# The first two matmuls of layer one on token halves, with two transposes meant to go between them

## The chip, the core and the metric

The kernel runs on one core of a Trainium2 chip. The metric is the device time of one execution in microseconds (us). The profile records one execution. It times from the first instruction of the program (the span, about 1.3 us shorter than the metric). TensorE has two rows in it: PE for matmuls and PEld for the weight loads that run under them (208.5 and 121.1 us busy in a span of 212.0 us, so they overlap). DVE is VectorE, ACT is ScalarE, SP is the engine that issues most loads (SPq in the lists).

## The reference, cut to what matters

For 2048 tokens of width 640 the program computes a gate, a state-space branch and a dense branch, and mixes them:

```python
x = A_x                                            # 1 x 2048 x 640
g = _sigmoid((x * gate_w).sum(-1, keepdims=True))
a = _A_ref(x, ...)        # x -> 640 complex states, scan over tokens, projection back
b = _B_ref(x, w1, b1, w2, b2)                      # gelu(x @ w1 + b1) @ w2 + b2, 640 -> 1728 -> 640
return g * a + (1 - g) * b
```

Only the first matrix product of `_B_ref`, "layer one", for the first 512 tokens is touched. It contracts over 640 input features, which are five slabs of 128. Each slab needs the matching rows of `w1` and the matching 128 rows of x transposed (features on partitions, tokens along the row).

## The kernel before

Every operation is declared with its inputs, its outputs, an assumed duration and a priority. A small list scheduler then decides each engine's order once, when the kernel is built. It does so from the *assumed* durations: at every step it takes, among the operations whose inputs are ready in its own clock, the one with the lowest priority number.

```python
def order(self):
    ...
        avail = [(it.prio, it.idx, it) for it, r in released[e] if r <= now + 1e-9]
        avail.sort(key=lambda x: (x[0], x[1]))
        it = avail[0][2]
```

The loads of the start are issued in this order. Slabs 0 and 1 of x are loaded plainly and transposed on TensorE. Slabs 2 to 4 come through a transposing load (`xtrans`).

```python
KN = 2
load("xna", "sp", "l_xna", xn[0][:, :, 0:KN * 128], ...)      # x, slabs 0 and 1
w1load(0, "sp", 1)
w1load(1, "sp", 1.3)
w1load(2, "sp", 2)
xtrans(0, range(KN, KD), 3, 1.8)                              # xT, slabs 2, 3, 4
w1load(3, "sp", 4)
w1load(4, "sp", 5)
```

A warm-up of six and a half empty matmuls keeps TensorE busy almost until x is there (in the profile of this kernel it starts at 0.78 us, its last matmul at 3.29, and the first transpose at 3.68). Then come eight 128x128 transposes into PSUM (where TensorE's results go, here eight banks `PS[0]` to `PS[7]`), three copies from PSUM to `xT`, and the forty matmuls of the first eight output tiles, slab by slab (`k`), eight tiles each (`jf`):

```python
for i, (k, c0, c1) in enumerate(((0, 0, 2), (0, 2, 4), (1, 0, 4))):   # slab, token blocks
    bank = 7 - i
    ...                                     # f_xt: TensorE transposes of these blocks into PSUM
    op(f"xt{i}", "pe", 0.11 * (c1 - c0), ["xna", "ident"], [("bank", bank)], f_xt, prio=-990 + i)
    ...                                     # f_xc: VectorE copies them to xT[0]
    op(f"xc{i}", "dve", 0.42, [("bank", bank)], [("xT", 0, k, c0)], f_xc, prio=-2000 + i)

def m1_first():
    seq = [(k, jf) for k in range(KD) for jf in range(NW)]
    seq.remove((0, NW - 1))
    seq.insert(seq.index((1, NW - 1)), (0, NW - 1))
    for k, jf in seq:

        def f_mm(jf=jf, k=k):
            return inc("pe", nc.tensor.matmul(PS[jf][:, :], W1sb[:, k, jf * 128:(jf + 1) * 128], xT[0][:, k, :],
                                              start=(k == 0), stop=(k == KD - 1)))

        op(f"m1_0_{jf}_{k}", "pe", d_mm(512), XK0[k] + [("w1", k)], [("bank", jf)], f_mm, prio=pe_prio())
```

The tile `jf = 7` of slab 0 is pushed behind the seven others of slab 1, because its PSUM bank 7 is first used for transposes.

Of the kernel before, what the change touches and what calls it, by code (L numbers as in the profile page):

```python
# [147 lines left out]
class Prog:  # L148
# [8 lines left out]
    def op(self, name, eng, dur, reads, writes, fn, prio=None, lat=0.0, after=()):  # L157
        deps = {}
        for k in reads:
            for w in self.last_w.get(k, ()):  # L160
                deps[w.idx] = w
        for k in writes:
            for w in self.last_w.get(k, ()):
                deps[w.idx] = w
            for r in self.last_r.get(k, ()):
                deps[r.idx] = r
        for a in after:
            deps[a.idx] = a
        deps = list(deps.values())
        E = self.E  # L170

        def run(eg, deps=deps, eng=eng, fn=fn):
            E.wait(eng, *[d.done for d in deps if not (eng == "pe" and d.eng == "pe")])
            return fn()

        it = self.sch.add(name, eng, dur, deps, run, prio=prio, lat=lat)
        for k in writes:
            self.last_w[k] = [it]
            self.last_r[k] = []
        for k in reads:  # L180
            self.last_r.setdefault(k, []).append(it)
        return it


def bass_gated_mix__ssm_conv_s5__dense_activation_gelu__prompt_kernel(
# [18 lines left out]
    _, S, D = A_x.shape  # L204
# [3 lines left out]
    KD = D // 128  # L208
# [17 lines left out]
    with ExitStack() as es:  # L226

        def SB(name, shape, dt):
            return es.enter_context(nc.sbuf_tensor(name, list(shape), dt))

        xT = [SB(f"xT_{i}", [128, KD, 512], BF16) for i in range(NQ)]
        xn = [SB(f"xn_{i}", [128, 4, D], BF16) for i in range(2)]
        W1sb = SB("W1sb", [128, KD, F], BF16)
# [9 lines left out]
        cols = SB("cols", [128, 3 * KP + NF], FP32)  # L243
# [10 lines left out]
        ident = SB("ident", [128, 128], BF16)  # L254
# [33 lines left out]
        PS = [es.enter_context(nc.psum_tensor(f"ps{i}", [128, 512], FP32)) for i in range(8)]  # L288
# [13 lines left out]
        op = pr.op  # L302

        def inc(eng, ins):
            return E.inc(eng, ins, eng + "_s")
# [8 lines left out]
        def d_act(n):  # L314
            return 0.26 + n * 0.00084
# [4 lines left out]
        def d_mm(n):  # L320
            return n / 2400.0 + 0.004
# [44 lines left out]
        ROWS = {"lre": (0, A_Lambda_re), "lim": (KP, A_Lambda_im), "ldt": (2 * KP, A_log_dt), "b1a": (3 * KP, B_b1[0:nmain])}  # L366
# [34 lines left out]

        op("warm", "pe", 2.7, (), [("bank", 4)], f_warm, prio=-1000)

        for i, (k, c0, c1) in enumerate(((0, 0, 2), (0, 2, 4), (1, 0, 4))):
            bank = 7 - i
            pt = PS[bank][:, :].bitcast(BF16)[:, 0:(c1 - c0) * 128]

            def f_xt(k=k, pt=pt, c0=c0, c1=c1):
                t = None
                for c in range(c0, c1):  # L410
                    t = nc.tensor.transpose(pt[:, (c - c0) * 128:(c - c0 + 1) * 128], xn[0][:, c, k * 128:(k + 1) * 128], ident[:, :])
                return inc("pe", t)

            op(f"xt{i}", "pe", 0.11 * (c1 - c0), ["xna", "ident"], [("bank", bank)], f_xt, prio=-990 + i)

            def f_xc(k=k, pt=pt, c0=c0, c1=c1):
                return inc("dve", nc.vector.tensor_copy(out=xT[0][:, k, c0 * 128:c1 * 128], in_=pt))

            op(f"xc{i}", "dve", 0.42, [("bank", bank)], [("xT", 0, k, c0)], f_xc, prio=-2000 + i)

        XK0 = [[("xT", 0, k)] for k in range(KD)]
        XK0[0] = [("xT", 0, 0, 0), ("xT", 0, 0, 2)]
        XK0[1] = [("xT", 0, 1, 0)]
        XT = {q: [("xT", q, k) for k in range(KD)] for q in range(1, NQ)}
        XT[0] = [t for x in XK0 for t in x]

# [2 lines left out]
        def f_cols():  # L429
            return inc("pe", nc.tensor.transpose(psC, rows[:, :], ident[:, :]))  # L430

        op("cols", "pe", 0.3, list(ROWS) + ["b1b", "ident"], [("bank", 7)], f_cols, prio=11.5)

        def f_cols1():
            return inc("dve", nc.vector.tensor_copy(out=cols[:, :], in_=psC[:, 0:RT + 1]))
# [147 lines left out]
        def pe_prio():  # L583
            ctr["pe"] += 1
            return ctr["pe"]
# [26 lines left out]
        def m1_first():  # L612
            seq = [(k, jf) for k in range(KD) for jf in range(NW)]
            seq.remove((0, NW - 1))
            seq.insert(seq.index((1, NW - 1)), (0, NW - 1))
            for k, jf in seq:

                def f_mm(jf=jf, k=k):
                    return inc("pe", nc.tensor.matmul(PS[jf][:, :], W1sb[:, k, jf * 128:(jf + 1) * 128], xT[0][:, k, :],  # L619
                                                      start=(k == 0), stop=(k == KD - 1)))  # L620

                op(f"m1_0_{jf}_{k}", "pe", d_mm(512), XK0[k] + [("w1", k)], [("bank", jf)] ,
                   f_mm, prio=pe_prio())
            for jf in range(NW):
                ctr["bank"] += 1

                def f_ge(jf=jf):
                    return inc("act", nc.scalar.activation(Gl[0][:, jf, :], PS[jf][:, :], ACT.Gelu_apprx_tanh, bias=b1col[:, jf:jf + 1]))

                op(f"ge_0_{jf}", "act", d_act(512), [("bank", jf), "b1col"], [("gl", 0, jf)], f_ge, prio=10)  # L630
# [248 lines left out]
        def outs(q, mid=None):  # L879
# [14 lines left out]
            comb(cs[-1])  # L894

        m1_first()
        m1(0, NW)
        bproj(0)
# [81 lines left out]
```

## Time and profile before

The time was 213.26 us (median of 3 runs).

The page of the profile, its first table and its summary of the chain that ended last (followed back from the last instruction, at each step to what released it):

```profile
span 212.0 us, 3133 instructions
PE 208.5 (98%) x1264; PEld 121.1 (57%) x1274; DVE 189.3 (89%) x263; ACT 111.3 (53%) x201; POOL 3.0 (1%) x11
...
PE 96%; DMA 2%; SPq 0%; issue 0%; DVE 0%
PE ps L769 27%; PE ps L639 22%; PE ps L818 21%; PE ps L682 20%; PE ps L619 3%; DMA W1sb<-in_B_w_dram 2%; PE ps L783 1%; PE ps L660 1%; SPq L326 0%; DVE osb L852 0%; PE ps L430 0%
```

The kernel is a row of matmuls. The only other thing on its chain of any size is a load of W1sb, 2% of the span. Line L619 is the matmul of the code above, the part that is changed, and it holds 3%.

The same chain in order of time for the start (start in us, length in us, what it was):

```profile
1.80 4.59 DMA W1sb<-in_B_w_dram
6.39 0.05 issue
6.44 1.04 PE ps L619 x4
...
8.61 0.04 issue
8.65 3.84 PE ps L619 x17
...
14.00 5.40 PE ps L639 x25
```

What lies before 6.39 us on TensorE is not on the chain at all: the chain goes through the load of W1sb slab 1. Twenty-five 512-column matmuls take 5.40 us, so one takes 0.216 us in this unbroken stretch.

The waits of the weight-load row (who waited for what, total us, times, longest), from 3 to 9 us:

```profile
PEld ps L411 <- DMA xn<-in_A_x_dram: 0.7, 1, 0.7
PEld ps L619 <- DMA W1sb<-in_B_w_dram: 0.6, 1, 0.6
PEld ps L619 <- DMA xT<-in_A_x_dram: 0.5, 1, 0.5
...
PEld ps L619 <- DVE xT L417: 0.2, 1, 0.2
```

So TensorE waits for x (until 3.68), for the second copy (until 4.68), for W1sb slab 1 (until 6.44), and for xT slab 2 (until 8.65). A weight load can be done before its matmul (the last one of slab 1 runs from 8.02 to 8.12 us, its matmul starts at 8.23), so these lengths on the weight-load row overstate the lost time. The matmul starts tell it better. The timeline in windows of a few hundredths of a microsecond shows the last matmul before each of the two later waits:

```profile
5.99 0.38 PE L619 MATMUL ps<-xT,W1sb 128*128 128x512 bf16 x1
8.23 0.38 PE L619 MATMUL ps<-xT,W1sb 128*128 128x512 bf16 x1
```

The first wait costs 6.44 - (5.99 + 0.216) = 0.23 us and the second 8.65 - (8.23 + 0.216) = 0.20 us. Whatever is delayed ahead of both waits has 0.43 us of slack in this run.

### The profile page before, as it was taken

The numbers are of one execution on the slowest core, as the hardware profiler recorded it, in microseconds if no ns is written. First come the engines' busy times: TensorE is split into PE (matmuls) and PEld (weight loads), VectorE is DVE, ScalarE is ACT, GpSimd is POOL, SyncE is SP. The second block draws the span as 40 slices with busy tenths as digits, with TensorE's granted clock in tenths as the row PEclk, the third lists the DMA queues.
The fourth block names the chain that finished last, engine by engine and source line by source line (L and its number), as shares of the span: only waits on it lengthen the run. The fifth ranks groups of instructions, "written<-read, shape, count | busy, mean of one in ns | idle before, by whom it ended". The sixth has DMA issues, their size and how long they took to land.

```text
span 212.0 us, 3133 instructions
## 1 busy us (share of the span) xinstructions
PE 208.5 (98%) x1264; PEld 121.1 (57%) x1274; DVE 189.3 (89%) x263; ACT 111.3 (53%) x201; POOL 3.0 (1%) x11
## 2 busy tenths in 40 slices
PE   8999999999999999999999999999999999999996
PEld 3344444444467776444466777544446777767775
DVE  2499999999999999999999959899999999899544
ACT  2489556678915234556953233556793444723331
POOL 2000000000000010000000001000000000000000
PEclk9999999999999999999999999999999999999999
DMA  5999799999100004100000014000000000010011
GB/s 151 310 276 206 157 231 317 261 203 180 21 0 3 31 31 127 62 0 0 0 3 0 0 34 156 31 31 3 0 0 2 3 31 31 31 34 0 31 34 62
DMA packets 31318, 16.35 MB, mean 77 GB/s; under 512 B 23112, under 2 KB 30408, under 8 KB 31304
## 3 DMA queue, kind: packets, MB, share of 16 engines
q1 hardware_dynamic: 30928, 14.83, 28.4%
q0 software_dynamic: 320, 1.31, 1.9%
q8 instruction: 10, 0.16, 0.3%
q14 instruction: 4, 0.03, 0.1%
q10 hardware_dynamic: 56, 0.01, 0.0%
HBM read 7.63 MB, written 2.62 MB: 48 GB/s over the span
## 4 chain that ended last, share of the span: by engine, by line
PE 96%; DMA 2%; SPq 0%; issue 0%; DVE 0%
PE ps L769 27%; PE ps L639 22%; PE ps L818 21%; PE ps L682 20%; PE ps L619 3%; DMA W1sb<-in_B_w_dram 2%; PE ps L783 1%; PE ps L660 1%; SPq L326 0%; DVE osb L852 0%; PE ps L430 0%
## 5 line engine op out<-in xcount | busy, mean ns | idle before, releaser
L769 PE MATMUL ps<-W2sb,Gl 128*128 128x320 bf16 x416 | 59.2, 299 | 0.0
L769 PEld LDWEIGHTS ps<-W2sb,Gl 128*128 128x128 bf16 x416 | 40.4, 98 | 17.0 <-issue 1.1
L639 PE MATMUL ps<-xT,W1sb 128*128 128x512 bf16 x215 | 47.5, 379 | 0.3
L818 PE MATMUL ps<-CT,H 128*128 128x320 bf16 (+2 forms) x330 | 45.4, 295 | 0.0
L722 DVE TENSOR_TENSOR_SCAN W<-atab,V 128x1280 bf16<-128x1280 f32 x16 | 44.3, 2811 | 0.3
L682 PE MATMUL ps<-xT,BT 128*128 128x512 bf16 x196 | 43.1, 379 | 0.3 <-issue 0.2
L818 PEld LDWEIGHTS ps<-CT,H 128*128 128x128 bf16 x330 | 32.0, 98 | 11.7
L797 ACT ACTIVATE E<-ps,g1col 128x320 bf16<-128x320 f32 x32 | 16.3, 526 | 39.7 <-PE ps L769 25.8
L639 PEld LDWEIGHTS ps<-xT,W1sb 128*128 128x128 bf16 x220 | 21.6, 98 | 25.9
L646 ACT ACTIVATE Gl<-ps,cols 128x512 bf16<-128x512 f32 x44 | 29.6, 689 | 10.0 <-PE ps L639 10.0
L682 PEld LDWEIGHTS ps<-xT,BT 128*128 128x128 bf16 x200 | 19.5, 98 | 23.4 <-ACT Gt L668 0.4
L691 ACT ACTIVATE U<-ps 128x512 bf16<-128x512 f32 x40 | 23.8, 597 | 14.9 <-PE ps L682 14.9
L829 ACT ACTIVATE E<-ps,gcol 128x320 bf16<-128x320 f32 x30 | 15.8, 528 | 22.6 <-PE ps L818 22.6
L756 ACT ACTIVATE ps<-b2b 128x320 f32<-128x320 bf16 x32 | 14.1, 442 | 1.1
L480 DVE TENSOR_TENSOR osb<-xg,E 128x640 bf16<-128x640 bf16 x15 | 7.3, 487 | 8.1 <-ACT E L829 7.8
L839 DVE SCALAR_TENSOR_TENSOR xg<-xn,gcol,dsk 128x640 bf16<-128x640 bf16 x16 | 13.9, 883 | 0.4
L596 DVE SCALAR_TENSOR_TENSOR scr<-xn,gwb 128x640 bf16<-128x640 bf16 x16 | 13.2, 823 | 0.4
L480 DVE TENSOR_TENSOR H<-H,V 128x1280 bf16<-128x1280 bf16 x16 | 12.5, 821 | 0.3
L480 DVE TENSOR_TENSOR V<-V,W 128x1280 bf16<-128x1280 bf16 x16 | 12.5, 821 | 0.3
L480 DVE TENSOR_TENSOR V<-mr,U 128x2560 bf16<-128x2560 bf16 x8 | 11.9, 1489 | 0.2
L480 DVE TENSOR_TENSOR H<-c,W 128x2560 bf16<-128x2560 bf16 x8 | 11.9, 1489 | 0.2
L480 DVE TENSOR_TENSOR V<-s,W 128x2560 bf16<-128x2560 bf16 x8 | 11.9, 1484 | 0.0
(80 smaller groups left out, 100.0 us busy)
## 6 DMA issues: line engine op xcount, KB each, us to landing
out_dram<-osb SPq DMA_DIRECT2D x15, 160.0 KB, 1.8
W2sb<-in_B_w_dram SPq DMA_DIRECT2D x1, 2080.0 KB, 9.2
W1sb<-in_B_w_dram SPq DMA_DIRECT2D x5, 256.0 KB, 4.6
xn<-in_A_x_dram POOLq DMA_DIRECT2D x2, 640.0 KB, 4.7
xn<-in_A_x_dram SPq DMA_DIRECT2D x1, 640.0 KB, 8.3
W1sb<-in_B_w_dram SPq DMA_DIRECT2D x1, 480.0 KB, 5.5
W1sb<-in_B_w_dram SPq DMA_DIRECT2D x1, 400.0 KB, 6.3
xn<-in_A_x_dram SPq DMA_DIRECT2D x1, 384.0 KB, 6.0
```

The lines of the kernel that those rows point to most:

```text
L480: return inc("dve", nc.vector.tensor_tensor(out=o, in0=a, in1=b, op=o_))
L639: t = nc.tensor.matmul(PS[bank][:, :], W1sb[:, k, jf * 128:(jf + 1) * 128], xT[q][:, k, :], start=(k == 0), stop=(k == KD - 1))
L646: return inc("act", nc.scalar.activation(Gl[q % 2][:, jf, :], PS[bank][:, :], ACT.Gelu_apprx_tanh, bias=b1col[:, jf:jf + 1]))
L682: t = nc.tensor.matmul(PS[bank][:, :], BT[:, ci, kd, k * 128:(k + 1) * 128], xT[q][:, kd, :], start=(kd == 0), stop=(kd == KD - 1))
L691: return inc("act", nc.scalar.activation(dst, src, ACT.Copy, scale=1.0 if ci == 0 else -1.0))
L722: t = inc("dve", nc.vector.tensor_tensor_scan(out=g[:, ci, :], data0=a, data1=v[:, ci, :], initial=0.0, op0=ALU.mult, op1=ALU.add))
L756: return inc("act", nc.scalar.activation(PS[bank][:, 0:HALF], b2b[:, cols], ACT.Copy))
L769: t = nc.tensor.matmul(PS[bank][:, 0:HALF], Gl[q % 2][:, jf, t4 * 128:(t4 + 1) * 128], W2sb[:, jf, cols], start=False, stop=False, skip_gr ...
L797: return inc("act", nc.scalar.activation(E1[c % NE][:, cols], PS[bank][:, 0:HALF], ACT.Copy, scale=g1col[:, c:c + 1]))
L818: t = nc.tensor.matmul(PS[bank][:, 0:n], H[b % NHB][:, ci, k, s * 128:(s + 1) * 128], CT[:, ci, k, cols], start=(i == 0), stop=(i == 2 * K ...
L829: return inc("act", nc.scalar.activation(E2[c % NE][:, cols], PS[bank][:, 0:HALF], ACT.Copy, scale=gcol[:, c:c + 1]))
L839: return inc("dve", nc.vector.scalar_tensor_tensor(out=xg[c % 2][:, :], in0=xn[q % 2][:, c % 4, :], scalar=gcol[:, c:c + 1], in1=dsk[:, :] ...
```

## The change

The first two matmuls (tiles 0 and 1 of slab 0) are cut into token halves. The first halves need only the first copy, so they could start before the second copy is done. To fit, the four transposes of slab 1 are cut in two pairs. The second pair goes to bank 7 again, once the first copy has emptied it, and has a priority that should place it between the first and second halves. Of the two halves of a tile only the first carries the `start` flag.

```diff
-        for i, (k, c0, c1) in enumerate(((0, 0, 2), (0, 2, 4), (1, 0, 4))):
-            bank = 7 - i
+        for i, (k, c0, c1) in enumerate(((0, 0, 2), (0, 2, 4), (1, 0, 2), (1, 2, 4))):
+            bank = (7, 6, 5, 7)[i]
...
-            op(f"xt{i}", "pe", ..., f_xt, prio=-990 + i)
+            op(f"xt{i}", "pe", ..., f_xt, prio=(-990, -989, -988, 2.5)[i])
...
-        XK0[1] = [("xT", 0, 1, 0)]
+        XK0[1] = [("xT", 0, 1, 0), ("xT", 0, 1, 2)]
...
-        op("cols", "pe", 0.3, ..., f_cols, prio=11.5)
+        op("cols", "pe", 0.3, ..., f_cols, prio=13.5)
...
-            for k, jf in seq:
-                ... matmul(PS[jf][:, :], W1sb[...], xT[0][:, k, :], start=(k == 0), stop=(k == KD - 1))
+            steps = [(0, 0, 0), (0, 1, 0), (0, 0, 1), (0, 1, 1)] + [(k, jf, None) for k, jf in seq if k or jf > 1]
+            for k, jf, h in steps:
+                t0, t1 = (0, 512) if h is None else (256 * h, 256 * h + 256)
+                ... matmul(PS[jf][:, t0:t1], W1sb[...], xT[0][:, k, t0:t1],
+                           start=(k == 0 and t0 == 0), stop=(k == KD - 1), skip_group_check=jf < 2)
```

More of the change, by code (lines that the diff above doesn't have):

```diff
@@ L412, in f_xt @@
                 return inc("pe", t)
-            op(f"xt{i}", "pe", 0.11 * (c1 - c0), ["xna", "ident"], [("bank", bank)], f_xt, prio=-990 + i)
+            op(f"xt{i}", "pe", 0.11 * (c1 - c0), ["xna", "ident"], [("bank", bank)], f_xt, prio=(-990, -989, -988, 2.5)[i])
             def f_xc(k=k, pt=pt, c0=c0, c1=c1):
@@ L430, in f_cols @@
             return inc("pe", nc.tensor.transpose(psC, rows[:, :], ident[:, :]))
-        op("cols", "pe", 0.3, list(ROWS) + ["b1b", "ident"], [("bank", 7)], f_cols, prio=11.5)
+        op("cols", "pe", 0.3, list(ROWS) + ["b1b", "ident"], [("bank", 7)], f_cols, prio=13.5)
         def f_cols1():
@@ L615, in m1_first, with f_mm @@
             seq.insert(seq.index((1, NW - 1)), (0, NW - 1))
-            for k, jf in seq:
-                def f_mm(jf=jf, k=k):
-                    return inc("pe", nc.tensor.matmul(PS[jf][:, :], W1sb[:, k, jf * 128:(jf + 1) * 128], xT[0][:, k, :],
-                                                      start=(k == 0), stop=(k == KD - 1)))
-                op(f"m1_0_{jf}_{k}", "pe", d_mm(512), XK0[k] + [("w1", k)], [("bank", jf)] ,
+            steps = [(0, 0, 0), (0, 1, 0), (0, 0, 1), (0, 1, 1)] + [(k, jf, None) for k, jf in seq if k or jf > 1]
+            for k, jf, h in steps:
+                t0, t1 = (0, 512) if h is None else (256 * h, 256 * h + 256)
+                def f_mm(jf=jf, k=k, t0=t0, t1=t1):
+                    return inc("pe", nc.tensor.matmul(PS[jf][:, t0:t1], W1sb[:, k, jf * 128:(jf + 1) * 128], xT[0][:, k, t0:t1],
+                                                      start=(k == 0 and t0 == 0), stop=(k == KD - 1), skip_group_check=jf < 2))
+                op(f"m1_0_{jf}_{k}_{t0}", "pe", d_mm(t1 - t0), (XK0[k] if h is None else XK0[k][h:h + 1]) + [("w1", k)], [("bank", jf)],
                    f_mm, prio=pe_prio())
```

## The prediction

> **What bounds the kernel.** TensorE. The page gives PE 208.5 us busy of a 212.0 us span (98%), and the chain of waits puts 96% of the span on PE instructions, 2% on a DMA of W1sb. From 8.65 us to the end the chain is practically unbroken matmuls. VectorE (89%) is off the chain but for the last store. Only the first 8.65 us can react to this change.
>
> **The start of before (timelines in narrow windows).** xn lands at 3.68. Eight transposes issue at 3.68 to 4.41, about 0.107 us apart. The three copies to xT start at 4.12, 4.33 and 4.76 and take 0.29, 0.29 and 0.42 us. The first layer-one matmul starts at 4.68, released by the second copy (PEld idle 0.22 us). Matmuls then follow each other in about 0.215 us. But PE stops twice more, both times for a DMA (list of waits): 0.56 us on the weight-load row until 6.43, when the second W1sb slab lands (matmul start times leave about 0.22 us of that: the last matmul of slab 0 starts at 5.99), and 0.53 us until 8.64, when the transposed xT load lands (about 0.4 us real: last start about 8.02).
>
> **What the change does.** The intent is to start the first two matmuls on tokens 0-255 as soon as the first copy is done (4.41 us), not after the second (4.63): at most about 0.2 us earlier. Added: two 256-column matmuls in place of each of two 512-column ones (two more weight loads of 0.098 us, hidden, same columns streamed); one more copy on VectorE, two of 0.29 in place of one of 0.42 (+0.16 us in a stretch where VectorE idles until 7.57); and the last two transposes now write bank 7 again, so they wait for the first copy to empty it. The instruction order shows that the scheduler still puts all eight transposes before the first half matmul, so the intended interleaving does not happen: six transposes (last issue about 4.23), wait for copy one (4.41), two transposes at about 4.45 and 4.56, first half matmul at about 4.66. The second halves need copy two (4.63), which is there. So even the start is where it was, 4.68 within 0.1 us. The fourth copy should end near 5.2 us (estimate), long before slab 1 needs it at 6.43.
>
> **On the critical path: nothing.** A head start of 0.2 us would end in the wait at 6.43, a delay of up to 0.2 us too, and a further 0.4 us is absorbed at 8.64. The rest of all engines' orders is unchanged, line for line; the small column transpose stays between the fourth and fifth matmul of slab 1. [...]
>
> **Prediction.** 213.3 us, 8 in 10 between 212.8 and 213.8. Before's own runs spread from 213.12 to 213.81. Faster by over 2%: 0.005; within 2%: 0.99; slower by over 2%: 0.005.
>
> **What would show each step.** Last two transposes issue after 4.41, first half matmul at 4.6 to 4.75; the wait for the W1sb slab still ends near 6.4 and that for xT near 8.6, its length within 0.2 us of before's; the piece of the chain after 8.65 keeps its lengths.
>
> **What would make it wrong.** DMA landings moving by themselves (a few tenths); or the transposes' 0.107 us against the matmuls' half pace per column: columns are streamed twice as fast from about 4.6 us on, so if that switch came later by a microsecond[...], slab 0 would outlast both waits by some tenths. Either is under 1%.

Two passages of it are cut, marked above: a sentence on what the halves' flags do, and the reason that it gave for a later switch of TensorE's pace. No run or trace of this case shows either. The forecast itself loses no term by that: 213.3 us answers to the 213.26 us of the kernel before in its first three runs, with nothing added or taken off.

## The result, and the profile after

The changed kernel took 213.58 us (median of 6 runs, 213.32 to 213.92), the kernel before 213.66 us in the same rounds. The ratio is 1.0002, with a 95% interval of 0.9984 to 1.0019. Here and below a ratio is the mean time of one kernel's runs over the mean of the other's runs of the same rounds, so it is not quite the ratio of the medians quoted beside it.

The page after, the lines that answer to those of before:

```profile
span 212.1 us, 3138 instructions
PE 208.3 (98%) x1266; PEld 121.1 (57%) x1276; DVE 189.3 (89%) x264; ACT 111.3 (52%) x201; POOL 3.0 (1%) x11
...
PE 96%; DMA 2%; issue 0%; SPq 0%; DVE 0%
```

The chain after in order of time:

```profile
1.80 4.64 DMA W1sb<-in_B_w_dram
6.43 0.14 issue
6.57 1.02 PE ps L621 x4
...
7.65 4.42 PE ps L621 x20
...
14.01 5.40 PE ps L641 x25
```

By this chain the first forty matmuls of layer one end at 14.01 instead of 14.00 (the ends of matmuls are modelled; by its first matmul the ninth tile begins at 13.85 instead of 13.84). The time between is told by TensorE's timeline (start, length, engine, line, operation, count, and in brackets the idle time before). First the kernel before, then after:

```profile
3.68 1.04 PE L411 MATMUL ps<-ident,xn 128*128 128x128 bf16 x8
4.68 2.79 PE L619 MATMUL ps<-xT,W1sb 128*128 128x512 bf16 x11
...
13.84 5.56 PE L639 MATMUL ps<-xT,W1sb 128*128 128x512 bf16 x25
```

```profile
3.65 1.07 PE L411 MATMUL ps<-ident,xn 128*128 128x128 bf16 x8
4.56 1.68 PE L621 MATMUL ps<-xT,W1sb 128*128 128x256 bf16 x9
6.57 1.02 PE L621 MATMUL ps<-xT,W1sb 128*128 128x512 bf16 x4 [0.34 <-DMA W1sb<-in_B_w_dram]
...
13.85 5.56 PE L641 MATMUL ps<-xT,W1sb 128*128 128x512 bf16 x25
```

Narrow windows show the last matmul before each of the two waits after the change:

```profile
5.86 0.38 PE L621 MATMUL ps<-xT,W1sb 128*128 128x512 bf16 x1
8.35 0.38 PE L621 MATMUL ps<-xT,W1sb 128*128 128x512 bf16 x1
```

The eight transposes still form one block, so the interleaving did not happen. The first half matmul starts at 4.56 against 4.68. Of these 0.12 us, 0.03 come from x, which landed earlier in this run: counted from the first transpose it is 0.91 against 1.00 us. Part of the rest may come from the last two transposes, which start 0.07 us apart here (4.43 and 4.50) and 0.11 us apart in the kernel before (4.30 and 4.41; see e3), so the change's own share cannot be read from this pair. The head start of 0.12 us is still there at the end of slab 0: its last matmul starts at 5.86 against 5.99. Then it is gone. TensorE now waits 6.57 - (5.86 + 0.216) = 0.49 us for W1sb slab 1, where before it waited 0.23. It restarts 0.13 us *later* than before, because the load lands 0.04 later and because 0.14 us pass between landing and matmul, not 0.05. The weight load of slab 1 now also waits for the fourth copy. The chains of other runs show both lengths: 0.13 us in e4 at slab 1, 0.14 us in e2 at slab 3 and in all three e7 runs at the first transpose, but 0.05 us in e1 at slab 2. What decides between them was not shown; a second input alone does not, since slab 2 in e1 has two as well, xT and W1sb. That the split itself costs the 0.09 us here is the author's estimate and was not tested apart. That delay in turn disappears in the wait for xT slab 2. The last matmul of slab 1 starts at 8.35, so that wait has shrunk to 8.66 - (8.35 + 0.216) = 0.09 us. Slab 2 begins at 8.66 against 8.65.

### The profile page after: what moved, and what is told of

The parts are those of the page before. It is cut to its first block, busy times and chain, and to the rows that moved or that the text cites. A ratio compares the mean times of both kernels' runs of the same rounds, so it can differ in the third digit from the quotient of the medians. Undisturbed runs are those within 1.5% of the kernel's fastest.

```text
span 212.1 us, 3138 instructions
## 1 busy us (share of the span) xinstructions
PE 208.3 (98%) x1266; PEld 121.1 (57%) x1276; DVE 189.3 (89%) x264; ACT 111.3 (52%) x201; POOL 3.0 (1%) x11
## 3 DMA queue, kind: packets, MB, share of 16 engines
q0 software_dynamic: 320, 1.31, 2.0%
## 4 chain that ended last, share of the span: by engine, by line
PE 96%; DMA 2%; issue 0%; SPq 0%; DVE 0%
PE ps L771 27%; PE ps L641 22%; PE ps L820 21%; PE ps L684 20%; PE ps L621 3%; DMA W1sb<-in_B_w_dram 2%; PE ps L785 1%; PE ps L662 1%; SPq L326 0%; DVE osb L854 0%; PE ps L430 0%
```

## The experiments

The theory: the start of the kernel is set by the landing of the loads, so a head start of TensorE before them is worth nothing. The rivals: (a) TensorE's work adds up, and the change gave nothing because its head start was eaten by the added instructions; (b) it gave nothing only because the scheduler left the transposes in front.

One quantity makes the single traces comparable: the start of the first matmul of the ninth tile (line L639 before, with other line numbers in the variants). I call it the end of the start phase. In the kernel before it is 13.84 us and the profiled run took 213.35 us. In every one of the 14 profiled runs the time is this moment plus 199.50 to 199.57 us. The rest of the program thus ran off alike in all of them, and all differences between these runs, beyond 0.07 us, arose before that moment.

| run | time, median (range) | before beside it | ratio, 95% interval | slab 0 / 1 / 2 begin | end of start phase |
|---|---|---|---|---|---|
| before | 213.66 (213.12-213.90) | - | - | 4.68 / 6.44 / 8.65 | 13.84 |
| after | 213.58 (213.32-213.92) | 213.66 | 1.0002 (0.9984-1.0019) | 4.56 / 6.57 / 8.66 | 13.85 |
| e1_drop_slab0 | 213.34 (213.19-215.03) | 213.42 | 1.0024 (0.9993-1.0054) | none / 6.47 / 8.54 | 13.73 |
| e2_drop_slab2 | 212.85 (212.29-213.37) | 213.42 | 0.9972 (0.9956-0.9987) | 4.66 / 6.38 / none | 12.72 |
| e3_pad2 | 213.90 (213.32-214.35) | 213.42 | 1.0022 (1.0006-1.0037) | 5.46 / 7.41 / 9.41 | 14.59 |
| e3_pad8 | 214.88 (214.15-215.51) | 213.42 | 1.0067 (1.0049-1.0085) | 6.47 / 7.97 / 9.97 | 15.15 |
| e4_intended | 213.35 (213.18-213.55) | 213.48 | 0.9987 (0.9958-1.0017) | 4.58 / 6.50 / 8.61 | 13.80 |
| e5_split_before | 213.34 (213.10-213.65) | 213.48 | 0.9986 (0.9953-1.0019) | 4.81 / 6.89 / 8.89 | 14.07 |
| e5_split_intended | 213.25 (212.94-213.90) | 213.29 | 1.0004 (0.9986-1.0022) | 4.58 / 6.50 / 8.49 | 13.67 |
| e6_early_before | 213.62 (213.07-213.88) | 213.48 | 0.9997 (0.9966-1.0028) | 4.67 / 6.65 / 8.65 | 13.83 |
| e6_early_intended | 213.47 (213.21-213.60) | 213.48 | 0.9992 (0.9962-1.0022) | 4.64 / 6.50 / 8.50 | 13.68 |
| e7_late_before | 219.04 (218.77-219.56) | 213.68 | 1.0257 (1.0239-1.0274) | see below | 19.25 |
| e7_late_after | 219.17 (218.76-219.38) | 213.68 | 1.0258 (1.0241-1.0274) | see below | 19.25 |
| e7_late_intended | 219.22 (219.01-219.32) | 213.68 | 1.0259 (1.0245-1.0274) | see below | 19.69 |

The numbers of a trace come from the profiled run alone. The medians come from all runs. Beside e4, e5_split_before and both e6, one run of the kernel before took 215.52 us, 1.8 us more than the next longest. It raises the mean that these four are divided by: without it the ratios of the plain means would be 0.9997, 0.9997, 1.0006 and 1.0001.

### e1 and e2: the same work taken out before and behind the waits

```diff
 def f_mm(jf=jf, k=k):
+    if k == 0:                      # e2: k == 2
+        return None
     return inc("pe", nc.tensor.matmul(...,
-                                      start=(k == 0), stop=(k == KD - 1)))
+                                      start=(k == 1), stop=(k == KD - 1)))      # e2: unchanged
```

The sums are wrong. The comparison with the reference passed all the same, so it is too coarse to see one missing slab of layer one. The orders of all engines stay as they were.

> The kernel before without its eight matmuls of slab 0 (wrong sums on purpose; 8 x 0.216 = 1.7 us of TensorE work less, all but one of them ahead of the first of the two waits). Theory (the two DMA waits at 6.4 and 8.6 us set the start, whatever ran before them): wait for the xT load still ends at 8.5 to 8.8, total unchanged, 213.6 within 0.4. Rival (TensorE's work adds up, so any earlier start is worth its length, and the change gave nothing because its head start was too small or was eaten by the added half matmuls): total about 211.9, 1.7 us less.

> Control: the same amount of work (eight matmuls, 1.7 us) taken out just behind the wait for the xT load, in slab 2, wrong sums on purpose. Theory: total falls by 1.0 to 1.7 us (less than 1.7 if the W1sb slab 3, which lands near 9.3 by its issue at 4.65 plus 4.6, becomes the next wait). Rival: falls by 1.7 us, just as the removal of slab 0 would.

The chain of e1, which lacks the 1.7 us of slab 0 (eight matmuls, seven of them ahead of the first wait):

```profile
2.78 5.71 DMA xT<-in_A_x_dram
8.50 0.05 issue
8.54 5.35 PE ps L621 x24
```

Slab 2 begins at 8.54 instead of 8.65, just because the load came 0.1 us earlier in this run (it landed at 8.50 us and its weight load starts at 8.54, against 8.64 in the kernel before). The time did not fall (213.34 beside 213.42; ratio 1.0024). Two of its six runs were 1.6 us longer than the rest (214.82 and 215.03), which raises the mean. One of them lists a granted clock of 0.992; they have no trace and stay unexplained. The other four have a mean of 213.28 beside 213.45, far from 1.7 us less. For e2 the chain is:

```profile
4.47 4.66 DMA W1sb<-in_B_w_dram
9.13 0.14 issue
9.27 3.61 PE ps L621 x16
```

The same eight matmuls taken out *behind* the waits move the end of the start phase from 13.84 to 12.72 us. It would have been 1.7 us, but the next load, W1sb slab 3, now sets the pace: it lands at 9.13. The mean time falls by 0.28% (0.6 us), which is clear of noise, though less than the 1.0 us expected and less than the profiled run shows (212.29 against 213.35). Why the other runs gained less was not found. What the pair settles: taking work out ahead of the waits gains nothing that can be told from noise, taking it out behind them does. An earlier start by 0.1 or 0.2 us cannot count where 1.7 us do not. Rival (a) falls.

### e3: a later start, to measure the slack

```diff
+def f_pad():
+    for _ in range(2):              # e3_pad8: 8
+        t = nc.tensor.matmul(PS[4][:, :], one.broadcast_to([128, 128]), one.broadcast_to([128, 512]), start=True, stop=True)
+    return inc("pe", t)
+op("pad", "pe", 0.2, ["xna"], [("bank", 4)], f_pad, prio=-900)
```

> The kernel before with two empty 512-column matmuls on constants between the last transpose and slab 0: first layer-one matmul 0.3 to 0.5 us later. Theory: swallowed by 0.2 us of wait at 6.4 and 0.4 us at 8.6; total unchanged, 213.6 within 0.3, and the xT wait still ends at 8.6 with a shorter length. Rival (no slack, work adds up): 0.3 to 0.5 us more.

> Same with eight empty matmuls: first layer-one matmul about 1.6 to 1.8 us later. Theory: the slack of 0.6 us is used up, both waits are gone, total 0.9 to 1.2 us more (214.5 to 214.8). Rival: 1.6 to 1.8 us more.

With eight empty matmuls slab 0 starts 6.47 - 4.68 = 1.79 us later, and the start phase ends 15.15 - 13.84 = 1.31 us later. So 0.48 us were swallowed, which fits the 0.43 us of the two waits. The time rose by 0.67% (1.4 us), a little more than expected.

Two empty matmuls should have been swallowed whole, and were not: +0.22%, about 0.5 us. The weight-load row of the profiled run (start, length, and idle time before) shows why in that run:

```profile
5.04 0.15 PEld L627 LDWEIGHTS ps<-xT,W1sb 128*128 128x128 bf16 x1 [0.28 <-DVE xT L417]
5.47 0.15 PEld L627 LDWEIGHTS ps<-xT,W1sb 128*128 128x128 bf16 x1 [0.27 <-issue]
...
6.32 1.62 PEld L627 LDWEIGHTS ps<-xT,W1sb 128*128 128x128 bf16 x8 [0.28 <-issue]
```

Up to 6.3 us one matmul follows the other in 0.43 us, twice the 0.216 us of later. I call the first half pace and the second full pace. The two pads then cost 0.85 us and not 0.43, and slab 0 is slowed as well. In the profiled run of the kernel before, the half pace had ended by 4.7 us. This is not a property of the variant: kernels whose TensorE instructions up to slab 0 are the same (before and e2, or e7_late_before and e7_late_after up to the end of the warm-up) show it at different times. The table gives the starts of two TensorE instructions between which the pace changes; the time from one start to the next tells the pace.

| profiled run | half pace ends between (us) |
|---|---|
| e2_drop_slab2 | 3.85 and 3.91 |
| e4_intended | 3.91 and 3.98 |
| e7_late_after | 3.72 and 4.05 |
| before | 4.41 and 4.68 |
| after | 4.16 and 4.50 |
| e7_late_before, e7_late_intended | 4.57 and 4.81 |
| e3_pad8 | 4.56 and 4.93 |
| e5_split_intended | 4.77 and 5.03 |
| e6_early_intended | 5.15 and 5.21 |
| e6_early_before | 5.50 and 5.79 |
| e5_split_before | 5.64 and 6.02 |
| e3_pad2 | 6.32 and 6.54 |

(In e1 it is not dated: the eight transposes from 3.82 us on take 0.94 us, and TensorE has nothing to do until 6.47, when the pace is full.) At half pace a matmul of 128 columns takes 0.107 us and one of 512 columns 0.43 us; at full pace it is 0.055 and 0.216 us. Counted from the first warm-up matmul, which starts at 0.78 us, the half pace ended after 3.1 to 5.8 us, and in e7, where the warm-up is unbroken, after 2.9 to 4.0 us. The column for the granted clock says 1.00 throughout, so the change of pace cannot be read there. What ends the half pace was not shown.

Where the half pace ended late, TensorE and not the loads can set the start. In the profiled run of e5_split_before, where it ended between 5.64 and 6.02 us, the chain has no load in it between the arrival of x and slab 2:

```profile
3.82 1.03 PE ps L412 x8
4.85 3.06 PE ps L620 x11
7.92 0.06 PE ps L431
7.97 6.26 PE ps L620 x29
```

### e4: the interleaving as it was meant

The scheduler had put the last two transposes in front because in its clock they become ready before the first W1sb slab. With that slab as a further input they fall behind the first halves.

```diff
-op(f"xt{i}", "pe", ..., ["xna", "ident"], [("bank", bank)], f_xt, ...)
+op(f"xt{i}", "pe", ..., ["xna", "ident"] + ([("w1", 0)] if i == 3 else []), [("bank", bank)], f_xt, ...)
```

> The kernel after, with the last two transposes really placed between the first and the second halves, as the change's words say (they are given the first W1sb slab as a further input, so the scheduler can't put them first). Theory: first half matmul at about 4.43 instead of 4.56, but the waits for W1sb slab 1 (6.4) and for xT (8.6) end where they did; total unchanged, 213.6 within 0.3. Rival (the change gave nothing because the scheduler left the transposes ahead): about 0.15 us less, and the whole chain after 8.6 earlier by that.

The transposes are now between the halves:

```profile
4.58 0.38 PE L621 MATMUL ps<-xT,W1sb 128*128 128x256 bf16 x2 [0.21 <-DVE xT L417]
4.79 0.27 PE L411 MATMUL ps<-ident,xn 128*128 128x128 bf16 x2
4.90 2.62 PE L621 MATMUL ps<-xT,W1sb 128*128 128x256 bf16 x11
```

x landed 0.14 us later in this run than in before's, so 4.58 and not 4.43 is the start. Slab 1 begins at 6.50, slab 2 at 8.61, the end of the start phase is 13.80 against 13.84. The ratio of 0.9987 is not clear of noise. Its interval rules out neither the theory nor 0.15 us. The trace fits the theory: the first wait ends 0.13 us after W1sb slab 1 lands (6.36), and the weight load of slab 2 waits for the xT load until 8.61.

### e5 and e6: taking the waits away

e5 splits the transposing load in two, with a correct result. e6 moves it behind all W1sb slabs and feeds slabs 2 to 4 with xT slabs 0 and 1. Its sums are wrong.

```diff
-xtrans(0, range(KN, KD), 3, 1.8)
+xtrans(0, range(KN, KN + 1), 3, 0.6)           # e5
+xtrans(0, range(KN + 1, KD), 3.1, 1.2)         # e5
+xtrans(0, range(KN, KD), 5.5, 1.8)             # e6, with xT[0][:, k % 2, :] as the moving operand
```

> The kernel before, with the transposing load of xT slabs 2 to 4 split in two: slab 2 alone, then slabs 3 and 4. Correct result. Theory: slab 2 lands earlier than 8.6, the wait there shrinks by 0.2 to 0.4 us and the total by as much, unless W1sb slab 2 turns out to land no earlier. Rival (what limits is the sum of bytes, not which load comes first): no change.

> The kernel after with the transposes really between the halves and the transposing xT load split (slab 2 alone, then slabs 3 and 4): the version that the runs so far would favour, correct result. [...] Theory: if this profile has an early release (first transposes or first halves already at full pace), the wait for slab 2 is gone or ends by 8.3, and the total is 0.2 to 0.5 us below before; if the release is late again, no wait shows and the total is within 0.3 of before. Rival (bytes in flight set it): with an early release the wait moves to the W1sb slabs 2 or 3 and nothing is gained.

> The kernel before with the xT load moved behind all five W1sb slabs, and slabs 2 to 4 of the first eight tiles fed with xT slabs 0 and 1 instead (wrong sums on purpose), so that no matmul of the first forty waits for xT. Theory: the wait at 8.6 goes (0.4 us less, and up to 0.6 if W1sb slab 1 lands earlier too); total 213.0 to 213.3. Rival: no change.

> The same loads and the same wrong data with the truly interleaved halves of e4_intended. Theory: if W1sb slab 1 now lands before slab 0 is done, no DMA wait is left to swallow the head start, and this is 0.1 to 0.25 us below e6_early_before; if a wait for slab 1 remains, no difference. Rival (head starts are never worth anything): no difference in either case.

In e5_split_intended the split does bring xT slab 2 earlier: slab 2 begins at 8.49 us without a wait, so its weight load started at about 8.28 (an estimate by the 0.21 us that such a load runs ahead of its matmul, 8.02 to 8.23 in the profile before). In the kernel before the weight load of slab 2 waited for xT until 8.64. (e5_split_before reached slab 2 only at 8.89, so its trace says nothing on this.) In none of the four traces does TensorE wait for xT at the start of slab 2. But no total is clear of noise (0.9986, 1.0004, 0.9997, 0.9992, each to within 0.2 to 0.3%). In all four the half pace ended late, at 4.8 us or after, and TensorE reached slab 2 at 8.49 to 8.89 us, about when the unsplit load would have landed (8.50 us in e1). In three of them it ran without a break from slab 0 on. In e5_split_intended it still waited for W1sb slab 1, 6.50 - (6.16 + 0.216) = 0.12 us, and from there the 1.99 us of work to slab 2 were unbroken: with the xT wait gone, the load ahead of it sets the start, and the start phase ends 0.17 us before that of the kernel before. Expectations of 0.2 to 0.4 us less (e5_split_before, e6_early_before) were misses. That of e5_split_intended for a late "release" (its word for the moment at which the full pace sets in; the sentence on e5_split_before, which speaks of a clock, is cut) held: no wait for xT, total within 0.3 us. e6_early_intended lies 0.15 us below e6_early_before by the medians, as expected, but within noise. In the traces the two runs with the truly interleaved halves end the start phase at 13.67 and 13.68, the two others at 14.07 and 13.83. The half pace of these two with the halves ended earlier as well, so this can't be put down to the halves.

### e7: what the head start is worth where nothing swallows it

In e7 the start is held back until all five W1sb slabs are there and TensorE runs at full pace (the warm-up matmuls are 0.22 us apart from 4.81 us on at the latest).

```diff
-for n in (512,) * 6 + (256,):
+for n in (512,) * 28:
-op(f"xt{i}", "pe", ..., ["xna", "ident"], ...)
+op(f"xt{i}", "pe", ..., ["xna", "ident", ("w1", KD - 1)], ...)
```

In e7_late_before the column transpose gets the second copy as a further input, so that the order stays the same. In e7_late_after the transposes are kept in front by priority, as in the kernel after.

> The kernel before with its start held back: 28 warm-up matmuls instead of six and a half, and the first transposes wait for the last of the five W1sb slabs, so that when layer one begins no load is outstanding[...]. Correct result. All theories: 5 to 7 us longer than before, a first layer without any wait. If the spread of the ordinary kernels (213.0 to 213.9) comes from loads[...], the runs of this one should lie closer together, within about 0.3 us. It is the base for the two runs beside it.

> The kernel after in the order as built (all eight transposes first), start held back the same way. Theory (the head start is real but small, and in the ordinary kernel is swallowed by waits for loads): from the first transpose to the first half matmul about 0.1 us shorter than in e7_late_before, and the end of layer one earlier by the same 0.1 us. Rival (splitting costs what it gains: two more matmuls, two more weight loads, one more wait): no difference or slower.

> The same with the transposes really between the halves. Theory: from the first transpose to the first half matmul 0.2 us shorter than in e7_late_before, and 0.15 to 0.25 us less at the end of layer one. Rival: no difference.

TensorE's timelines from the first transpose to the ninth tile, e7_late_before, e7_late_after, e7_late_intended:

```profile
9.70 0.61 PE L411 MATMUL ps<-ident,xn 128*128 128x128 bf16 x8 [0.78 <-DMA W1sb<-in_B_w_dram]
10.55 2.55 PE L619 MATMUL ps<-xT,W1sb 128*128 128x512 bf16 x11 [0.25 <-DVE xT L417]
...
19.25 5.56 PE L639 MATMUL ps<-xT,W1sb 128*128 128x512 bf16 x24
```

```profile
9.78 0.49 PE L411 MATMUL ps<-ident,xn 128*128 128x128 bf16 x6 [1.19 <-DMA W1sb<-in_B_w_dram]
10.43 0.28 PE L411 MATMUL ps<-ident,xn 128*128 128x128 bf16 x2 [0.16 <-DVE xT L417]
10.55 2.54 PE L621 MATMUL ps<-xT,W1sb 128*128 128x256 bf16 x13
...
19.25 5.56 PE L641 MATMUL ps<-xT,W1sb 128*128 128x512 bf16 x24
```

```profile
10.21 0.49 PE L411 MATMUL ps<-ident,xn 128*128 128x128 bf16 x6 [1.30 <-DMA W1sb<-in_B_w_dram]
10.87 0.39 PE L621 MATMUL ps<-xT,W1sb 128*128 128x256 bf16 x2 [0.16 <-DVE xT L417]
11.10 0.28 PE L411 MATMUL ps<-ident,xn 128*128 128x128 bf16 x2
...
19.69 5.56 PE L641 MATMUL ps<-xT,W1sb 128*128 128x512 bf16 x24
```

| | first transpose to first layer-one matmul | first transpose to ninth tile |
|---|---|---|
| e7_late_before | 10.55 - 9.70 = 0.85 | 19.25 - 9.70 = 9.55 |
| e7_late_after | 10.55 - 9.78 = 0.77 | 19.25 - 9.78 = 9.47 |
| e7_late_intended | 10.87 - 10.21 = 0.66 | 19.69 - 10.21 = 9.48 |

As built, the head start is 0.08 us and stays 0.08 us. With the true interleaving it is 0.19 us, but only 0.07 us are left at the ninth tile. The expected 0.15 to 0.25 us was wrong, and the lines show the reason. The last two transposes (0.11 us from 11.10 to 11.21) used to run while TensorE waited for the copies anyway. Moved between the halves, they stand in the stream of matmuls. So even without any load in the way the idea is worth 0.08 us, 0.04% of the time, in one trace of each kernel and at full pace; at half pace it was not measured. Rival (b) falls with it, as far as these traces go: the scheduler's order cost nothing that the interleaving would have won.

The three totals do not differ (1.0257, 1.0258, 1.0259). Their runs spread over 0.8, 0.6 and 0.3 us, so the expectation of a narrower spread held for one of three. The load that the start waits for moved as well: the last W1sb slab landed at 9.56, 9.64 and 10.08 us in the three profiled runs. That the moment of full pace and the landings of the loads are what spreads the *ordinary* kernel by 0.9 us is the author's estimate from this and from the table above, and was not shown. Shown is that in the profiled runs the whole difference lies in the start phase.

## Why the prediction was right

The time was right: 213.3 us predicted with 212.8 to 213.8, 213.58 measured. The kernel before alone gave 213.66 over six runs and 213.26 over the three that the prediction had, so the 0.3 us between point and result say nothing of the mechanism, and landing in a range as wide as the kernel's own spread proves little. What the runs test is the steps. Point by point:

- *"On the critical path: nothing."* Right, and shown by e1: 1.7 us taken out ahead of the waits gave no gain clear of noise, while the same work taken out behind them gained 0.6 us (e2).
- *The scheduler leaves all eight transposes in front.* Right. The first half matmul came at 4.56 us, just outside the predicted 4.6 to 4.75, because the last two transposes took 4.56 - 4.43 = 0.13 us and not 0.21: TensorE was at full pace by 4.50 us in that run.
- *"a further 0.4 us is absorbed at 8.64"* was mis-sized. The prediction took 8.02 us for the start of the last matmul before that wait. It is 8.23, so the wait costs 0.20 us, and both waits together give 0.43 us of slack and not 0.6. e3_pad8 measured 0.48 us.
- *The length of each wait within 0.2 us of before's.* The second held (0.09 against 0.20). The first grew from 0.23 to 0.49 us, by 0.26 us, since slab 0 ended 0.13 us earlier and slab 1 began 0.13 us later.
- That the halves' flags give correct sums is not shown.
- *A later switch of the matmuls' pace* was named as a risk. It came at anything from 3.9 to 6.3 us over the profiled runs, and the latest three of those that can be dated (e3_pad2, e5_split_before, e6_early_before) are all kernels without the halves. One trace of each kernel is too little to say more. In e3_pad2 and e5_split_before no load stands on the chain between the arrival of x and slab 2, so there the head start could count. By the 0.08 us of e7 it would be some 0.1 us, an estimate, since e7 ran at full pace.
- *The rest of the program runs off as before.* Right, to within 0.07 us in all 14 profiled runs.

No version with a correct result is shown to beat both kernels. e5_split_intended, the best on paper, gave 213.25 us beside 213.29. One thing was not tried: loads that land earlier together with a full pace that sets in earlier, which might shorten the start phase.

## What to carry to other kernels

Before making an engine start earlier, look for the next wait on its row that ends at a load's landing. Here, as long as that load and not the engine came last, a head start before it gained nothing: 1.7 us taken out ahead of it gave no gain clear of noise (e1), the same behind it 0.6 us (e2). In e3_pad2, at half pace up to 6.32 us, the engine came last. Deleting the work outright (e1) against deleting as much behind the wait (e2) is a cheap test of it. Count a moved instruction against the idle time that it leaves: in e7 the last two transposes ran in a wait for copies, and took 0.11 us of the stream of matmuls once they were moved into it. Where single runs spread by more than the effect, find one moment in the trace after which all runs are alike, and compare at that moment.
